# A gate projection by seven block products in two more token groups, with q of the last two batches weighted on ScalarE

One core of a Trainium2 chip. The metric is the device time of one execution in microseconds (us), median of several; smaller is better.

## The reference

Linear attention with a cosine weighting, then a SwiGLU block, all of it in one kernel:

```python
# q, k, v: (8 batches, 8 heads, 576 tokens, 64)
def phi(x, c, s):                       # c, s: cos and sin of pi/2 * position / 576
    r = np.maximum(x, 0.0)
    return np.concatenate([r * c, r * s], axis=-1)
kv  = einsum('bhsf,bhsd->bhfd', phi(k), v);  z = sum(phi(k), axis=2)
num = einsum('bhsf,bhfd->bhsd', phi(q), kv); den = phi(q) . z + 1e-6
x   = (num / den) -> (4608 tokens, 512)
g   = x @ w_gate                        # 512 x 1536
out = (silu(g) * (x @ w_val)) @ w_out   # 1536 x 512
```

## The kernel before

It works on nine groups of 512 tokens, 0 to 8. A group has a **gate stage** (gate and value projections, silu, product into `ht`; 12 slots, 0 to 11) and an **output stage** (4 slots, 12 to 15). The attention for coming groups is hung into these slots: `at(slot, function)` appends work, and every engine runs its instructions in the order in which the program emits them.

An ordinary gate stage has 12 blocks like this one, each with two of the eight PSUM banks (the buffers into which TensorE writes its sums, and which it can't use again until they have been read):

```python
def ffn_fc(tg, fc):
    # TensorE: 4 matmuls for the gate, 4 for the value, 512 tokens each
    # ScalarE: sg = silu(gate bank)
    # VectorE: ht[:, fc] = sg * value bank        (frees both banks)
```

Groups 7 and 8 (`GATE = (7, 8)`) make the gate by a scheme of seven products of half-size blocks instead of eight. The sums of blocks are made by VectorE, and intermediate results stay in PSUM:

```python
for u in range(3):                                     # [cut to the order of work]
    product(a, u, A11, B11, True)                      # TensorE
    nc.scalar.copy(out=b, in_=a)                       # ScalarE seeds bank b
    product(e, u, W3, X3, True);  nc.scalar.copy(out=m7, in_=e)
    V(...);  done()                                    # a value block; then the slot's work
    product(b, u, W2, X2, False)
    nc.vector.tensor_tensor(out=c, in0=m7, in1=b, op=ALU.add)      # must read b ...
    product(a, u, A12, B21, False);  silu(u, 1, 0, a)
    V(...);  done()
    product(b, u, W1, X1, False)                                   # ... before this writes b
    nc.vector.tensor_tensor(out=m7, in0=m7, in1=b, op=ALU.add)
    ...
    product(c, u, A22, X4, False); silu(u, 0, 0, c);  V(...);  done()
    mul(u, 0, 0); mul(u, 1, 0)                         # VectorE: silu times value
    product(b, u, W4, B22, False); silu(u, 1, 1, b)
    ...
```

A tile of 128 tokens of x (`a_tile2`) is 8 or 16 small matmuls and then three VectorE operations, `x_den`, `x_rec` and `x_mul` (the normalisation). The path of q of a batch b:

```python
def phi_q(b, g):                       # one of four head pairs
    o = raws[b, "q"][:, g]
    relu_op("act", o, o)                                          # ScalarE
    nc.vector.tensor_tensor(out=st[b, "q"][:, g], in0=o..., in1=tab, op=ALU.mult)   # weights
def qturn_dma(b, e):                   # transposes st[b, "q"] into phit[b], on SyncE's queue
    ...
def load_behind(b):
    nc.gpsimd.tensor_copy(out=hold2, in_=phit[b - 1][0:1, :, 0, 0, 0])  # waits for batch b-1's transposes
    load(b, "q")
    if b > 3:
        load_kv(b)
...
for b in range(2, B):
    s0 = SLOTS * (b - 1);  p0 = s0 - SLOTS         # SLOTS = 16: p0 is the start of group b - 2
    fs, tq = [p0 + 12, p0 + 12] + [p0 + 11 + i for i in range(2, 8)], (p0 + 15, p0 + 16)
    #        q: slots 12, 12, 13, 14; k and v: from slot 15 on; transposes of q: slots 15 and 16
    at(p0 + 3 if b < 5 else p0 + 1, lambda b=b: load_behind(b))
```

## Time and profile before

| | before |
|---|---|
| time, median (range) | 316.83 us (316.31 to 316.89) |
| TensorE busy | 98% of the span |
| VectorE, ScalarE busy | 73%, 46% |
| granted clock of TensorE | 0.998 |

In the rows of the windows further down, the columns are: start and end, length, busy time (and count) of PE (TensorE matmuls), PEld (weight loads), DVE (VectorE), ACT (ScalarE) and POOL (GpSimd), granted clock (1.00 is TensorE's full clock), DMA share, GB/s. In the order of time: start, length, engine, line, operation, count, and in brackets how long the engine had been idle and what ended that. In the lists of waits: what waited <- for what, us in total, how many times, the longest.

### The profile page before, as it was taken

The numbers are of one execution on the slowest core, as the hardware profiler recorded it, in microseconds if no ns is written. First come the engines' busy times: TensorE is split into PE (matmuls) and PEld (weight loads), VectorE is DVE, ScalarE is ACT, GpSimd is POOL, SyncE is SP. The second block draws the span as 40 slices with busy tenths as digits, with TensorE's granted clock in tenths as the row PEclk, the third lists the DMA queues.
The fourth block names the chain that finished last, engine by engine and source line by source line (L and its number), as shares of the span: only waits on it lengthen the run. The fifth ranks groups of instructions, "written<-read, shape, count | busy, mean of one in ns | idle before, by whom it ended". The sixth has DMA issues, their size and how long they took to land.

```text
span 314.5 us, 6775 instructions
## 1 busy us (share of the span) xinstructions
PE 307.5 (98%) x2696; PEld 189.7 (60%) x2696; DVE 228.2 (73%) x458; ACT 143.4 (46%) x264; POOL 36.0 (11%) x62
## 2 busy tenths in 40 slices
PE   8899999999999999999999999999999999999994
PEld 4597455455444585548654764577456866687673
DVE  7873777697678888587748786778779478946772
ACT  7554545763335346334543454335533345324530
POOL 7855102000200200030003000300000000000000
PEclk9999999999999999999999999999999999999999
DMA  7999999996897994989495979598951160014004
GB/s 268 217 198 197 206 205 138 226 133 99 143 208 114 150 145 110 148 119 196 100 153 75 200 144 154 73 192 135 164 86 35 40 145 17 20 38 98 0 2 133
DMA packets 74767, 41.07 MB, mean 131 GB/s; under 512 B 49904, under 2 KB 69872, under 8 KB 74736
## 3 DMA queue, kind: packets, MB, share of 16 engines
q1 hardware_dynamic: 51952, 22.55, 38.0%
q0 software_dynamic: 22192, 17.57, 37.2%
q10 hardware_dynamic: 592, 0.52, 0.5%
q8 instruction: 21, 0.34, 0.4%
q14 instruction: 10, 0.08, 0.1%
HBM read 37.75 MB, written 9.44 MB: 150 GB/s over the span
## 4 chain that ended last, share of the span: by engine, by line
PE 91%; DVE 5%; ACT 2%; issue 1%; ACTq 0%
PE banks L564 46%; PE banks L786 20%; PE banks L729 6%; PE banks L633 5%; PE banks L621 5%; PE banks L333 3%; PE banks L448 3%; DVE ht L638 1%; PE banks L494 1%; PE banks L430 1%; DVE v L287 1%; DVE sums L760 1%; DVE x L471 1%; PE banks L197 1%; PE banks L536 0%
## 5 line engine op out<-in xcount | busy, mean ns | idle before, releaser
L564 PE MATMUL banks<-xT,wg_sb 128*128 128x512 f16 (+2 forms) x368 | 86.6, 360 | 0.0
L564 PE MATMUL banks<-xT,wv_sb 128*128 128x512 f16 (+2 forms) x368 | 86.6, 360 | 0.0
L570 ACT ACTIVATE sg<-banks 128x512 bf16<-128x512 f32 (+2 forms) x92 | 51.5, 560 | 76.0 <-PE banks L564 74.0
L575 DVE TENSOR_TENSOR ht<-sg,banks 128x512 f16<-128x512 bf16 (+2 forms) x92 | 57.9, 637 | 29.7 <-PE banks L564 22.7
L564 PEld LDWEIGHTS <-wv_sb 128*128 128x128 f16 x368 | 35.5, 98 | 37.4
L564 PEld LDWEIGHTS <-wg_sb 128*128 128x128 f16 x368 | 33.9, 98 | 31.5 <-issue 0.2
L786 PEld LDWEIGHTS <-ht 128*128 128x128 f16 x336 | 32.5, 98 | 4.2
L786 PEld LDWEIGHTS <-sums 128*128 128x128 f16 x252 | 24.5, 98 | 4.2 <-issue 0.8
L633 PE MATMUL banks<-xT,wv_sb 128*128 128x512 f16 x96 | 24.3, 379 | 0.0
L283 DVE TENSOR_TENSOR r_q<-raw_q,tab 128x1152 bf16<-128x1152 bf16 x24 | 17.6, 754 | 7.4 <-ACT raw_q L266 7.1
L729 PE MATMUL banks<-wo_sb,ht 128*128 128x512 f16 x96 | 22.7, 379 | 0.0
L471 DVE TENSOR_TENSOR x<-banks,rec 128x512 f16<-128x512 f32 (+1 forms) x32 | 21.6, 674 | 1.3 <-PE banks L430 0.3
L786 PE MATMUL banks<-wo_sb,ht 128*128 128x256 f16 x168 | 20.6, 273 | 0.0
L287 DVE TENSOR_TENSOR v<-raw_v,tab 128x1152 bf16<-128x1152 bf16 x27 | 19.9, 751 | 0.5 <-ACT raw_v L849 0.5
L786 PE MATMUL banks<-wt_sb,sums 128*128 128x256 f16 x168 | 19.8, 273 | 0.1
L786 PE MATMUL banks<-wt_sb,ht 128*128 128x256 f16 x168 | 19.5, 273 | 0.0
L799 ACT ACTIVATE ob<-banks 128x512 f32<-128x512 f32 x14 | 8.4, 597 | 21.9 <-PE banks L786 21.9
L638 DVE TENSOR_TENSOR ht<-sg,banks 128x512 f16<-128x512 bf16 x24 | 15.5, 681 | 2.4 <-ACT sg L627 2.4
L266 ACT ACTIVATE raw_k<-raw_k 128x576 bf16<-128x576 bf16 (+1 forms) x25 | 17.1, 694 | 0.0
L998 POOL COPY hold<-phit 1x2 bf16<-1x2 bf16 x5 | 1.4, 287 | 129.3 <-DMA phit<-r_q 129.3
L760 DVE TENSOR_TENSOR sums<-ht 128x1024 f16<-128x1024 f16 (+1 forms) x28 | 15.5, 553 | 0.4
L266 ACT ACTIVATE raw_q<-raw_q 128x576 bf16<-128x576 bf16 x24 | 15.4, 675 | 0.0
(121 smaller groups left out, 334.6 us busy)
## 6 DMA issues: line engine op xcount, KB each, us to landing
out_dram<-ob SPq DMA_DIRECT2D x67, 128.0 KB, 2.5
raw_k<-in_k_dram POOLq DMA_DIRECT2D x7, 576.0 KB, 8.8
raw_q<-in_q_dram POOLq DMA_DIRECT2D x6, 576.0 KB, 6.0
raw_v<-in_v_dram POOLq DMA_DIRECT2D x6, 576.0 KB, 11.4
wo_sb<-in_moe_w_out_dram POOLq DMA_DIRECT2D x3, 512.0 KB, 12.8
wg_sb<-in_moe_w_gate_dram POOLq DMA_DIRECT2D x5, 256.0 KB, 9.4
wv_sb<-in_moe_w_val_dram POOLq DMA_DIRECT2D x5, 256.0 KB, 9.5
wo_sb<-in_v_dram SPq DMA_DIRECT2D x2, 576.0 KB, 4.0
```

The lines of the kernel that those rows point to most:

```text
L266: nc.scalar.activation(out=out, in_=in_, func=AF.Relu)
L283: nc.vector.tensor_tensor(out=st[b, "q"][:, g], in0=o.unsqueeze(2).to_broadcast([P, NC, 2, D]), in1=tab, op=ALU.mult)
L287: nc.vector.tensor_tensor(out=v2s[b == 1][:, g, :, :, 0:D], in0=(first if b == 0 and g == 0 else {"v": raw_of(b, "v")})["v"][:, g].unsquee ...
L471: nc.vector.tensor_tensor(out=st["x", t].rearrange("p (y e d) -> p e y d", e=2, d=D)[:, :, ys], in0=ps[:, :, 0:2 * J * D1].rearrange("p e ...
L564: nc.tensor.matmul(out=st["f", tg, fc, lo][i], lhsT=(wg_sb, wv_sb)[i][:, kc, fs], rhs=xT[tg][:, ts, kc], start=(kc == 0), stop=(kc == KC - 1))
L570: nc.scalar.activation(out=sg[:, 0:n], in_=st["f", tg, fc, lo][0], func=AF.Silu, scale=DOWN)
L575: nc.vector.tensor_tensor(out=ht[:, fc, r:r + n], in0=st.pop(("s", tg, fc, lo))[:, 0:n], in1=ps[1], op=ALU.mult)
L633: nc.tensor.matmul(out=val[u, i, w], lhsT=wv_sb[:, kc, fc * P:(fc + 1) * P], rhs=xT[tg][:, :, kc], start=(kc == 0), stop=(kc == KC - 1))
L638: nc.vector.tensor_tensor(out=ht[:, fc], in0=gates[u, w][:, i], in1=val.pop((u, i, w)), op=ALU.mult)
L729: nc.tensor.matmul(out=o_ps[t], lhsT=ht[:, fc, r:r + P], rhs=wo_sb[:, fc], start=(fc == 0), stop=(fc == FC - 1))
L760: nc.vector.tensor_tensor(out=o[:, lo:hi], in0=x[:, lo:hi], in1=y[:, lo:hi], op=op)
L786: nc.tensor.matmul(out=to[i][:, 0] if len(to) == 2 else to[0][:, i], lhsT=a[:, kc, i * P:(i + 1) * P], rhs=b[:, kc], start=first and kc == ...
```

## The change

Its intent: groups 5 and 6 use seven products too, which takes away an eighth of the gate's matmul work there. VectorE, which must do the extra additions, is relieved: q of batches 6 and 7 is weighted by ScalarE, by 18 relus a batch with a scale for each partition. The relus of k and the weighting of v of these batches move to the output stages, the copies of kv to ScalarE, one token sum to the output stage, and the tiles in front of seven-product groups to odd slots.

```diff
-    GATE = (7, 8)
+    PHI_ACT = 6
+    GATE = (5, 6, 7, 8)
...
+    def phi_q_part(b, c, w):
+        if (b, "q") not in st:
+            st[b, "q"] = rel.tile([P, G, NC, 2, D], BF16, name="r_q")
+        nc.scalar.activation(out=st[b, "q"][:, :, c, w], in_=raws[b, "q"][:, :, c], func=AF.Relu,
+                             scale=csk[:, c, w:w + 1])
...
-        for w, eng in enumerate((nc.scalar.copy, nc.vector.tensor_copy)):
+        for w, eng in enumerate((nc.scalar.copy, nc.scalar.copy if b - 1 in GATE else nc.vector.tensor_copy)):
...
-                token_sum(*((3, 0, 4) if u == 1 else (4, 0, 4)))
+            if u == 1:
+                token_sum(3, 0, 4)
...
-        token_sum(4, 4, 6)
+        token_sum(4, 0 if tg in GATE else 4, 6)
...
-        steps = [lambda b=b, g=g: phi_q(b, g) for g in range(G)]
+        steps = [lambda b=b, g=g: phi_q(b, g) for g in range(G)] if b < PHI_ACT else []
...
+            if b >= PHI_ACT:
+                for c in range(NC):
+                    at(p0 + 6 + c, lambda b=b, c=c: (phi_q_part(b, c, 0), phi_q_part(b, c, 1)))
+                fs = [p0 + 12, p0 + 12, p0 + 13, p0 + 15]
...
-            elif tg - 1 in GATE:
-                s = SLOTS * (tg - 1) + ((1, 2, 7, 9) if tg < 6 else (1, 2, 4, 7) if tg < 8 else (1, 2, 5, 6))[i]
+            elif tg in GATE:
+                s = SLOTS * (tg - 1) + ((1, 3, 7, 9) if tg < 6 else (1, 3, 5, 7))[i]
```

## The prediction

> **What bounds the kernel now.** I read the page first, then the chain that ended last, then the windows of each token group, then the order of time inside groups 4, 5 and 7.
>
> ```profile
> PE 307.5 (98%) x2696; PEld 189.7 (60%) x2696; DVE 228.2 (73%) x458; ACT 143.4 (46%) x264; POOL 36.0 (11%) x62
> PE 91%; DVE 5%; ACT 2%; issue 1%; ACTq 0%
> ```
>
> TensorE is busy for 98% of the span and holds 91% of the chain. The chain in order of time gives the group boundaries: group 4 runs from 152.70 us, 5 from 185.32, 6 from 217.83, 7 from 250.26, 8 from 281.13. The windows between them (length, then busy time of PE, PEld, DVE, ACT, POOL):
>
> ```profile
> 152.70:185.32 32.62, 32.59 (x294) 19.46 (x292) 24.14 (x46) 14.85 (x27) 2.40 (x4) 1.00 0.83 140
> 185.32:217.83 32.51, 32.48 (x285) 19.70 (x286) 24.74 (x47) 14.85 (x27) 2.91 (x4) 1.00 0.87 141
> 217.83:250.26 32.43, 32.43 (x295) 19.69 (x293) 23.13 (x45) 12.27 (x22) 0.00 (x0) 1.00 0.49 86
> 250.26:281.13 30.87, 30.37 (x251) 22.07 (x249) 22.95 (x45) 12.26 (x22) 0.00 (x0) 1.00 0.24 52
> ```
>
> Groups 4 to 6 are TensorE without a gap. Group 7, which already uses seven products, has 0.5 us of gaps, all of them waits for VectorE. So time comes only from matmul work taken away, as long as nobody makes TensorE wait. Who could? The change lets ScalarE read q earlier, so I looked at when q arrives (order of time, group 4, then group 5, then the q tile's landing times):
>
> ```profile
> 165.56 0.60 ACT L570 ACTIVATE sg<-banks 128x512 bf16<-128x512 f32 x1 [0.51 <-PE banks L564]
> 167.28 0.60 ACT L570 ACTIVATE sg<-banks 128x512 bf16<-128x512 f32 x1 [1.13 <-PE banks L564]
> ...
> 169.65 0.18 POOL L998 COPY hold<-phit 1x2 bf16<-1x2 bf16 x1 [31.01 <-DMA phit<-r_q]
> 170.10 0.74 POOL L131 DMA_DIRECT2D raw_q<-in_q_dram  x1 [0.28 <-PE banks L564]
> ...
> 179.11 1.25 ACT L266 ACTIVATE raw_q<-raw_q 128x576 bf16<-128x576 bf16 x2
> ```
> ```profile
> 201.50 0.73 POOL L998 COPY hold<-phit 1x2 bf16<-1x2 bf16 x1 [29.16 <-DMA phit<-r_q]
> 202.17 0.74 POOL L131 DMA_DIRECT2D raw_q<-in_q_dram  x1
> ```
> ```profile
> DMA to landing us min/median/max: 5.8/6.0/6.0
> ```
>
> The first line shown is the seventh silu of group 4 (slot 6). The load of batch 6's q goes out at 170.10, because the copy before it waits for the transposes of batch 5, and these stand in the queue behind the stores of group 3 (151.86 to 157.7). It lands at 170.10 + 6.0 = 176.1. Today ScalarE first touches it at 179.11 (slot 12): just in time. Batch 7's lands at 202.17 + 5.8 = 208.0, 22.7 us after group 5 began, and is first used at 211.62.
>
> **What the Trainium skill says.** "TensorE: Matmul & The Clock Gate", section "Architectural detail": the queues of ScalarE and VectorE are strict FIFO, so one instruction that waits for a DMA holds up all behind it. The trace agrees as far as it shows: in every group the order of time is the program's order. Same page, "What's actually happening": after about one idle window of 3.4 us TensorE's clock goes to half, and it takes a busy window to come back. In this trace the granted clock is 1.00 in every group, and 0.88 in the mean only in the last 4.5 us, when TensorE has nothing to do. No pause inside the run is long enough to test it. Same page, "Wait — 56ns, not 53.3ns?": N/2.4 GHz plus 2.5 ns for each matmul. The trace agrees: 48 matmuls of 512 columns took 10.36 us, 216 ns each, and 84 of 256 took 9.28 us, 110 ns each. "ScalarE: Activation LUTs", "What ACT_TABLE_LOAD costs": 186 ns + 0.833 ns per element, 93 ns more for a pointer scale, and 93 ns of overlap between neighbours. The 128x576 relu (675 ns; formula 666) agrees.
>
> **The change part by part.**
>
> Gate by seven products in groups 5 and 6. Out: 48 matmuls x 216 ns = 10.37 us. In: 84 x 108 ns = 9.07. TensorE saves 1.30 us a group, 2.6 in all. VectorE gains six adds of 0.69 and four token sums of 0.42 (5.8 us a group); ScalarE gains six copies of 0.58 (3.5). With 23 to 25 us and 12 to 15 us busy in 32.5, both can carry that by total. The two weight sums that stood in group 5 move earlier (0.95 us each, beside TensorE work).
>
> q of batches 6 and 7. Out: 4 relus x 0.675 = 2.7 us of ScalarE and 4 products x 0.754 = 3.0 of VectorE for each batch. In: 18 scaled relus of 256 elements at 186 + 93 + 213 = 492 ns, less 93 of overlap: 0.40 each, 7.2 us of ScalarE (estimates from the skill's formula). As an amount this is harmless. As a place it is not: the first pair stands at slot 6 of groups 4 and 5, the old ones stood at slot 12, and neither the load nor what it waits for is moved.
>
> Group 4, step by step. ScalarE finishes silu 6 at 166.2 and meets the first scaled relu, whose q lands at 176.1: 9.9 us blocked. TensorE goes on while it has banks: blocks 7, 8 and 9 (1.73 each, two banks each) and a tile (0.26, two banks) fill all eight at about 173.4. Silu 7 starts at 176.1 + 0.8 = 176.9, its product on VectorE ends at 178.2, and only then is there a bank: TensorE idle for about 5 us. VectorE then has eight operations in a row to go to the product of block 10 (products and token sums of 0.6, two tile normalisations of 1.06), which the output stage needs for its first matmuls: 178.2 + 5.7 = 183.9, against 175.8 now. **Loss 8.1 us.**
>
> Group 5, from its own start. q lands at +22.7 as before, since the whole chain of stores, transposes and load hangs on the end of group 4. Slot 6 comes after 14 product blocks (0.435), 7 value blocks (0.865), the key-value product (1.18) and three tiles (0.26): 14.1, with small waits 14.8. TensorE can do 2.0 us more (two product blocks, a value block, a tile) until +16.8 and then needs ScalarE's copy that seeds bank b. That comes after q and the first pair: 22.7 + 0.8 + 0.57 = 24.1. **Loss 7.3 us**; with the queue of relus behind it, 7.7; less the 1.3 saved, some 6.5 to 6.8 net.
>
> Cold clock. Both pauses are longer than one window, so I expect half speed for 3.4 to 6.8 us after each; where VectorE is the limit anyway this costs less. My estimate is 1 us in group 4 and 2 in group 5, from the page's window alone.
>
> Group 6 gains its 1.3 less about 0.3 of new waits: -1.0. Group 7: its tiles at slots 1 and 2 follow each other closely, and TensorE waits:
>
> ```profile
> 257.20 0.60 PE L621 MATMUL banks<-kvt,wgs_sb 128*128 128x256 f16 x4 [0.35 <-DVE x L471]
> 267.65 0.31 PEld L621 LDWEIGHTS <-wgs_sb 128*128 128x128 f16 x3 [0.36 <-issue]
> ```
>
> Its parts add up to 9.07 + 10.37 + 9.17 + 1.05 = 29.7 against 30.87 measured. Odd slots and one token sum (0.68) moved to the output stage should bring back half of it: -0.6. Group 8: 0. v in output stages: batch 6's v lands at 171.57 + 11.9 = 183.5; VectorE would meet it at about 181 if nothing else were late, but is 8 us late itself, so no wait is added.
>
> Sum: +8.1 + 6.7 + 3.0 - 1.0 - 0.6 = +16.2; I take two off for work that the queues let TensorE do after all: +14, that is **331 us**.
>
> **The rivals.** First, no block: if q came before slot 6, only the saving would be left, 316.83 - 2.6 - 0.6 + 0.5 = 314.1, within 2%. For it: the author tuned the slots, and ScalarE has half its time free. Against it: the landing of q follows from stores and transposes that the diff doesn't touch. Second, the block is there but mostly hidden: at the least, 9.9 less 5.4 of run-ahead in group 4 and 5.9 in group 5 stay, no cold clock, the savings in full: about 316.8 + 4.5 + 5.9 - 3.8 = 323.4. Third, VectorE becomes the bound of the gate stages: 12 products of 0.68, 6 adds of 0.69, 4 tiles of 1.06 and token sums of 3.3 make 19.9 us beside 20.5 to 21.7 of TensorE. It would eat the saving: 316 to 317. It is tight but under, and group 7 shows how small the waits are.
>
> **Range and chances.** 324 is the second rival with a little added, 338 the full sum with the cold clock at its longest in both groups. I give nine in ten to the block (slower by over 2% means above 323.2), one in eleven to the first or third rival, one in a hundred to over 2% faster: the whole matmul saving is under 1%.
>
> **What would show it.** In the profile of the changed kernel: ScalarE idle for some 10 us in group 4 and 8 in group 5 in front of the scaled relu, released by the q load; TensorE idle for 5 and 7 us there; granted clock under 1.00 in those slices; groups 4 and 5 near 41 to 43 and 39 to 41 us long, group 6 near 31.4, group 7 near 30.3. Wrong if the load of q is issued well before 165 us, or if ScalarE runs silus past the waiting relu; then the time is near 314.

## More of the kernel before

The weighted q (`r_q`) has one buffer, the raw q three.

## The result, and the profile after

The changed kernel took **337.35 us** (336.33 to 337.89, 4 runs) beside 316.82 us for the kernel before on the same chip: ratio 1.0648, 95% interval 1.062 to 1.0676. A ratio here is the mean time of one kernel's runs over that of the other's of the same rounds, so it is not quite the ratio of the medians.

First the page of the changed kernel, the lines that answer to those of the prediction, and the row of the clock in 40 slices:

```profile
PE 312.1 (93%) x2768; PEld 198.8 (59%) x2768; DVE 230.7 (69%) x462; ACT 159.9 (48%) x308; POOL 35.7 (11%) x62
PEclk9999999999999999999996999859999999999999
PE 72%; DVE 10%; DMA 9%; SPq 3%; ACT 3%; issue 2%; POOL 0%; DVEq 0%; POOLq 0%; ACTq 0%
```

TensorE's share of the chain has fallen from 91% to 72%. DMA and SyncE's queue hold 12% of it; before they did not appear. The granted clock has two dips. The windows of groups 4 to 7:

```profile
152.70:195.40 42.70, 35.77 (x295) 20.58 (x293) 24.97 (x48) 20.78 (x43) 2.40 (x4) 0.92 0.65 107
195.40:238.75 43.35, 35.22 (x323) 24.26 (x321) 26.32 (x49) 23.69 (x50) 2.41 (x4) 0.88 0.64 106
238.75:271.38 32.63, 32.17 (x330) 23.19 (x329) 23.46 (x45) 13.86 (x27) 0.00 (x0) 1.00 0.51 85
271.38:302.40 31.02, 29.83 (x245) 21.66 (x244) 22.79 (x44) 12.23 (x22) 0.00 (x0) 1.00 0.24 52
```

Groups 4 and 5 are 10 and 11 us longer than before. Group 6, which should have become shorter, is 0.2 us longer. (The last window ends 0.4 us before group 8 starts; group 7 takes 31.6 us.) The order of time in group 4:

```profile
170.18 0.17 POOL L1006 COPY hold<-phit 1x2 bf16<-1x2 bf16 x1 [31.51 <-DMA phit<-r_q]
170.63 0.75 POOL L132 DMA_DIRECT2D raw_q<-in_q_dram  x1 [0.28 <-PE banks L455]
...
176.26 0.91 ACT L290 ACTIVATE r_q<-raw_q,cs_all 128x256 bf16<-128x256 bf16 x2 [9.84 <-DMA raw_q<-in_q_dram]
177.07 0.57 ACT L577 ACTIVATE sg<-banks 128x512 bf16<-128x512 f32 x1
...
177.68 0.69 DVE L582 TENSOR_TENSOR ht<-sg,banks 128x512 f16<-128x512 bf16 x1 [10.29 <-ACT sg L577]
177.70 0.29 PE L455 MATMUL banks<-kv,phit 128*128 128x65 bf16 x4 [3.75 <-ACT sg L577]
...
180.06 1.86 PE L571 MATMUL banks<-xT,wg_sb 128*128 128x512 f16 x4 [1.28 <-DVE x L478]
```

The chain is to be read from the first line down. The q load leaves when it left before. ScalarE stands for 9.84 us in front of the first scaled relu (L290). The silu (L577) and VectorE's product (L582) stand behind it, and TensorE behind them for want of a bank. The last line has four 512-column matmuls in 1.86 us where four took 1.03 before. The clock in short windows tells why:

```profile
176.00:178.00 2.00, 0.29 (x4) 0.19 (x4) 0.32 (x1) 1.74 (x5) 0.00 (x0) 1.00 1.21 209
178.00:180.00 2.00, 0.37 (x4) 0.25 (x4) 1.93 (x6) 2.00 (x6) 0.00 (x0) 0.62 1.21 207
180.00:182.00 2.00, 1.94 (x5) 0.71 (x5) 2.00 (x5) 1.00 (x3) 0.00 (x0) 0.50 1.13 205
182.00:184.00 2.00, 2.00 (x6) 0.75 (x5) 1.63 (x5) 1.39 (x3) 0.00 (x0) 0.50 0.01 2
184.00:186.00 2.00, 2.00 (x8) 0.75 (x7) 1.36 (x3) 0.56 (x2) 0.00 (x0) 0.68 0.33 66
186.00:188.00 2.00, 2.00 (x20) 1.72 (x18) 1.53 (x3) 1.23 (x4) 0.00 (x0) 1.00 0.00 0
```

The column after POOL is the clock. It falls to a half at about 178.5, between the two short pieces of work in the pause, and is back at about 185.3, some 5 us after TensorE set to work again for good (180.06). In group 5 the same happens in the seven-product stage:

```profile
212.31 0.74 POOL L132 DMA_DIRECT2D raw_q<-in_q_dram  x1 [0.28 <-issue]
...
218.90 0.91 ACT L290 ACTIVATE r_q<-raw_q,cs_all 128x256 bf16<-128x256 bf16 x2 [7.45 <-DMA raw_q<-in_q_dram]
219.72 0.57 ACT L656 COPY banks<-banks 128x512 f32<-128x512 f32 x1
...
220.34 1.01 PE L628 MATMUL banks<-kvt,wgs_sb 128*128 128x256 f16 x4 [6.97 <-ACT banks L656]
```

Here it is the copy that seeds bank b (L656) for which TensorE waits 6.97 us.

### The profile page after: what moved, and what is told of

Its sections match the earlier page's. It is cut to its first block, busy times and chain, and to the rows that moved or that the text cites. A ratio compares the mean times of both kernels' runs of the same rounds, so it can differ in the third digit from the quotient of the medians.

```text
span 336.1 us, 6942 instructions
## 1 busy us (share of the span) xinstructions
PE 312.1 (93%) x2768; PEld 198.8 (59%) x2768; DVE 230.7 (69%) x462; ACT 159.9 (48%) x308; POOL 35.7 (11%) x62
## 4 chain that ended last, share of the span: by engine, by line
PE 72%; DVE 10%; DMA 9%; SPq 3%; ACT 3%; issue 2%; POOL 0%; DVEq 0%; POOLq 0%; ACTq 0%
PE banks L571 27%; PE banks L794 18%; PE banks L640 8%; PE banks L628 7%; PE banks L737 6%; DMA phit<-r_q 5%; DMA raw_q<-in_q_dram 4%; SPq L313 2%; DVE ht L645 2%; PE banks L340 2%; PE banks L455 2%; DVE v L294 1%; SPq L719 1%; DVE x L478 1%; PE banks L501 1%
## 5 line engine op out<-in xcount | busy, mean ns | idle before, releaser
L571 PE MATMUL banks<-xT,wg_sb 128*128 128x512 f16 (+2 forms) x272 | 63.8, 361 | 1.3 <-DVE x L478 1.3
L582 DVE TENSOR_TENSOR ht<-sg,banks 128x512 f16<-128x512 bf16 (+2 forms) x68 | 41.5, 620 | 32.2 <-PE banks L571 15.1
L571 PE MATMUL banks<-xT,wv_sb 128*128 128x512 f16 (+2 forms) x272 | 63.0, 358 | 0.0
L577 ACT ACTIVATE sg<-banks 128x512 bf16<-128x512 f32 (+2 forms) x68 | 37.1, 546 | 50.4 <-PE banks L571 47.2
L640 PE MATMUL banks<-xT,wv_sb 128*128 128x512 f16 x192 | 49.9, 387 | 0.3 <-DVE ht L645 0.3
L571 PEld LDWEIGHTS <-wg_sb 128*128 128x128 f16 x272 | 25.2, 99 | 23.8 <-issue 3.0
L645 DVE TENSOR_TENSOR ht<-sg,banks 128x512 f16<-128x512 bf16 x48 | 30.8, 680 | 6.0 <-ACT sg L634 6.0
L628 PE MATMUL banks<-kvt,wgs_sb 128*128 128x256 f16 x144 | 22.5, 280 | 8.0 <-ACT banks L656 7.0
L628 PEld LDWEIGHTS <-wgs_sb 128*128 128x128 f16 x192 | 18.2, 99 | 17.6 <-issue 11.0
L640 PEld LDWEIGHTS <-wv_sb 128*128 128x128 f16 x192 | 19.1, 100 | 14.8 <-issue 1.8
L634 ACT ACTIVATE sg<-banks 128x512 bf16<-128x512 f32 x36 | 20.4, 590 | 15.0 <-PE banks L628 14.9
L794 PEld LDWEIGHTS <-sums 128*128 128x128 f16 x252 | 24.6, 98 | 3.8 <-issue 1.0
L290 ACT ACTIVATE r_q<-raw_q,cs_all 128x256 bf16<-128x256 bf16 x36 | 16.1, 498 | 17.3 <-DMA raw_q<-in_q_dram 17.3
L737 PE MATMUL banks<-wo_sb,ht 128*128 128x512 f16 x96 | 22.7, 379 | 0.0
L794 PE MATMUL banks<-wo_sb,ht 128*128 128x256 f16 x168 | 20.6, 273 | 0.0
L294 DVE TENSOR_TENSOR v<-raw_v,tab 128x1152 bf16<-128x1152 bf16 x27 | 19.5, 750 | 0.5 <-ACT raw_v L857 0.5
L794 PE MATMUL banks<-wt_sb,sums 128*128 128x256 f16 x168 | 19.5, 273 | 0.0
L794 PE MATMUL banks<-wt_sb,ht 128*128 128x256 f16 x168 | 19.5, 273 | 0.0
```

The costliest lines, as they stand in the source:

```text
L294: nc.vector.tensor_tensor(out=v2s[b == 1][:, g, :, :, 0:D], in0=(first if b == 0 and g == 0 else {"v": raw_of(b, "v")})["v"][:, g].unsquee ...
L571: nc.tensor.matmul(out=st["f", tg, fc, lo][i], lhsT=(wg_sb, wv_sb)[i][:, kc, fs], rhs=xT[tg][:, ts, kc], start=(kc == 0), stop=(kc == KC - 1))
L577: nc.scalar.activation(out=sg[:, 0:n], in_=st["f", tg, fc, lo][0], func=AF.Silu, scale=DOWN)
L582: nc.vector.tensor_tensor(out=ht[:, fc, r:r + n], in0=st.pop(("s", tg, fc, lo))[:, 0:n], in1=ps[1], op=ALU.mult)
L628: nc.tensor.matmul(out=to[:, i], lhsT=a[:, c, 2 * u + i], rhs=x[:, :, c], start=first and i == 0 and c == 0, stop=c == KH - 1, skip_group_ ...
L634: nc.scalar.activation(out=gates[u, w][:, :, j * HT:(j + 1) * HT], in_=src, func=AF.Silu, scale=DOWN)
```

## The experiments

The lengths of the stages come from the order of time of TensorE (the first matmul of each stage), one profile each, in us. G is a gate stage, O the output stage before it:

| run | time, median | G4 | O5 | G5 | O6 | G6 | G7 |
|---|---|---|---|---|---|---|---|
| before | 316.6 to 316.8 | 23.3 | 9.5 | 23.0 | 9.4 | 23.2 | 21.5 |
| after | 337.35 | 33.5 | 9.2 | 33.6 | 9.7 | 23.5 | 22.4 |
| e1 q late | 325.60 | 24.3 | 10.2 | 26.9 | 9.9 | 26.2 | 22.4 |
| e2 gate only | 320.90 | 24.7 | 9.4 | 24.8 | 9.7 | 23.7 | 22.4 |
| e3 slots only | 316.60 | 23.3 | 9.4 | 23.0 | 9.4 | 23.3 | 21.7 |
| e4 q early | 319.79 | 24.6 | 9.2 | 23.8 | 9.7 | 23.8 | 22.4 |
| e5 q only | 334.89 | 31.9 | 9.2 | 31.8 | 9.2 | 23.2 | 21.4 |
| e6 zeros in the pause | 335.04 | 33.3 | 9.2 | 30.6 | 9.7 | 24.0 | 21.8 |
| e7 early, old slots | 320.58 | 24.3 | 9.2 | 24.5 | 10.1 | 24.1 | 21.7 |
| e8 early, even slots | 320.24 | 23.3 | 9.2 | 24.6 | 9.7 | 24.4 | 22.8 |
| e9 early, slot 7 | 318.35 | 23.3 | 9.7 | 23.8 | 10.1 | 24.1 | 21.7 |
| e10 no normalisation | 314.44 | 23.3 | 10.2 | 22.3 | 9.7 | 22.6 | 20.6 |

(O5 stands between G4 and G5.) G8, seven products with no attention work beside them, took 19.5 us in every one, which is the sum of its matmuls, 9.07 + 10.37.

### e5: the q part alone

```diff
 # the kernel before, with phi_q_part, without the old four steps of q, and
+            if b >= PHI_ACT:                       # PHI_ACT = 6
+                for c in range(NC):
+                    at(p0 + 6 + c, ... phi_q_part(b, c, 0), phi_q_part(b, c, 1))
+                fs = fs[4:]                        # k and v stay in their slots
```

> The kernel before with one part of the change: q of batches 6 and 7 by 18 scaled relus on ScalarE at slots 6 to 14; seven products in groups 7 and 8 only, tiles and v where they were. Theory (the relu that stands in front of a q not yet landed costs about 10 us in each of two groups, with or without the seven products): 333 to 338 us, groups 4 and 5 both near 42.5 us, granted clock near 0.92 in both. Rival (group 5 stalls in the changed kernel because its seven-product stage needs ScalarE's copies; with ordinary blocks the banks carry TensorE over it): 326 to 329 us, group 5 near 33 us.

Measured: 334.89 us (334.54 to 335.22), ratio 1.0576 (1.0561 to 1.0592). Groups 4 and 5 took 41.1 and 41.0 us, 8.3 and 8.6 more than before. Who waited for whom in groups 4 to 6, ScalarE (first line) and TensorE (the others):

```profile
ACT r_q L290 <- DMA raw_q<-in_q_dram: 18.3, 2, 9.2
...
PE banks L455 <- ACT sg L577: 10.0, 2, 5.1
PE banks L571 <- DVE x L478: 2.5, 2, 1.3
```

So the relus on ScalarE at these slots cost 18.3 us by themselves (16.9 of it in these two groups), without any new seven-product stage. The rival falls: ordinary blocks carry TensorE over only part of the wait, and it stood idle 5 us in each group. The clock was 0.92 in both, as expected. My figure of 42.5 us a group was 1.4 too high.

### e4: the cause taken away, the relus left in place

```diff
-        nc.gpsimd.tensor_copy(out=hold2, in_=phit[b - 1][0:1, :, 0, 0, 0])
-        load(b, "q")
+        if b >= PHI_ACT:                           # behind x of the group before, not behind q of the batch before
+            nc.gpsimd.tensor_copy(out=hold2, in_=xT[b - 2][0:1, 3, 0, 0:2])
+            load(b, "q")
+        nc.gpsimd.tensor_copy(out=hold2, in_=phit[b - 1][0:1, :, 0, 0, 0])
+        if b < PHI_ACT:
+            load(b, "q")
```

> The changed kernel, all in its place, but the q loads of batches 6 and 7 wait for the last turned tile of the group before instead of for the turned q of the batch before; k and v loads as they were. Theory (the lateness of the q load is the cause): q lands some 20 us earlier; what stays is that the single buffer of weighted q is read by the transposes until about 170 us in group 4 and 16 us into group 5, so ScalarE waits about 3.5 us in group 4 and 1 to 2 in group 5, TensorE nearly nothing; granted clock 1.00 throughout; 315.5 to 319 us. Rival (place or amount of the scaled relus is the cause): still above 325 us.

Measured: 319.79 us (319.59 to 322.05), ratio 1.0115 (1.0079 to 1.0151), granted clock 1.00 in the profiled run. The changed kernel lost 20.5 us against the kernel before; this one loses 3.2 against the kernel before of its own call, so 17.3 are back, with the same instructions in the same slots but for a one-row copy on GpSimd for each load. q now leaves at 150.71, and the second wait that had been hidden under the first is seen:

```profile
150.71 0.75 POOL L132 DMA_DIRECT2D raw_q<-in_q_dram  x1
...
169.82 0.31 PE L455 MATMUL banks<-kv,phit 128*64 128x65 bf16 x7 [1.09 <-DMA phit<-r_q]
...
169.93 0.91 ACT L290 ACTIVATE r_q<-raw_q,cs_all 128x256 bf16<-128x256 bf16 x2 [3.38 <-DMA phit<-r_q]
```

ScalarE waits 3.38 us for the transposes that still read the single weighted-q buffer (3.5 expected), and 0.29 us in group 5 (1 to 2 expected); the banks carry TensorE over that. TensorE's own 1.09 us, for a tile that needs the turned q, is another matter (e7). The time was 0.8 us above the range, so something besides the load keeps this kernel above the one before.

### e1: the relus after the landing

```diff
-                    at(p0 + 6 + c, lambda ...
+                    at(p0 + 12 + c // 3, lambda ...
```

> The changed kernel with the 18 scaled relus of batches 6 and 7 moved from slots 6 to 14 to slots 12 to 14 (three chunks of q a slot), all else as changed. Theory (ScalarE stands in line behind a q that has not landed): no wait of ScalarE for the q load over 1 us, granted clock 1.00 in every group, groups 4 and 5 back at about 32.6 and 31.5 to 32.5 us, time 314 to 318 us. Rival (the added 4.5 us of ScalarE work a batch, or the fuller gate stages, cost the time wherever they stand): still above 325 us.

Measured: 325.60 us (325.29 to 326.15), ratio 1.0279 (1.0262 to 1.0296). The theory's wait is gone: ScalarE waits nowhere for q in groups 4 to 6. But its time missed, and the measured one lies in the rival's range (above 325). One reason stands in the trace: 18 relus (7.5 us) now crowd into the output stage with four relus of k and the stage's own copies. TensorE's waits from group 4's output stage to group 6, then ScalarE's order of time where group 5 begins (187.2):

```profile
PE banks L628 <- ACT banks L656: 4.9, 2, 2.6
```
```profile
184.42 2.49 ACT L290 ACTIVATE r_q<-raw_q,cs_all 128x256 bf16<-128x256 bf16 x6
186.81 0.68 ACT L267 ACTIVATE raw_k<-raw_k 128x576 bf16<-128x576 bf16 x1
187.39 0.58 ACT L807 ACTIVATE ob<-banks 128x512 f32<-128x512 f32 x1
187.86 2.50 ACT L290 ACTIVATE r_q<-raw_q,cs_all 128x256 bf16<-128x256 bf16 x6
190.26 0.68 ACT L267 ACTIVATE raw_k<-raw_k 128x576 bf16<-128x576 bf16 x1
190.83 0.59 ACT L656 COPY banks<-banks 128x512 f32<-128x512 f32 x1
```

The seeding copy could start when the first product of the stage ends, at about 187.8; it comes at 190.83. The two waits of this kind make 4.9 of the 9.0 us lost. How much of the loss needs the relus at all is not separated here: e2, further down, loses 4.3 us without them. Group 5's 26.9 us also contain a clock dip that only the profiled run has (mean clock 0.992; the other three 0.999 to 1.000 and 0.5 to 0.8 us shorter): after a pause of 2.3 us the clock was at a half from about 192.8 to 196.2, while a pause of 2.6 us in group 6 brought none. So the relus have no room at slots 12 to 14 as they had none at slot 6: too early they stand before their data, late they are too many.

### e6: what the half clock costs

```diff
+            if tg == 5 and u == 2:
+                warm = take(1, fills=True)
+                for _ in range(28):
+                    nc.tensor.matmul(out=warm, lhsT=zeros, rhs=<zeros, 512 columns>, start=True, stop=True)
             product(b, u, W2, X2, False)
```

> The changed kernel with 28 matmuls of zeros (216 ns each, 6.0 us) put into TensorE's queue in group 5 at the point where it waits 7.0 us for ScalarE's copy; nothing else. Theory (the half clock after the pause costs 2 us and more by itself): the granted clock stays 1.00 in group 5 except for at most a us or two, the work from the copy to the output stage shrinks from 8.5 to 6 to 6.6 us, time 2.0 to 2.8 us under the changed kernel's 337.35: 334.5 to 335.4. Rival (after the pause ScalarE and VectorE set the pace, so the clock doesn't matter): 337 to 338.

Measured: 335.04 us (334.44 to 338.24), ratio 1.0602 (1.055 to 1.0653), 2.3 us under the changed kernel's median, though on another chip; the kernel before took 316.60 there and 316.82 here. One of the four executions took 338.24, and the intervals of the two ratios overlap, so it is the stage in the profile, and not the whole time, that shows the gain. The stretch from the copy to the output stage shrank from 8.5 us (220.34 to 228.86) to 5.6 (220.16 to 225.79). The same window of both, the changed kernel first:

```profile
220.00:226.00 6.00, 5.66 (x22) 3.19 (x22) 2.48 (x4) 3.41 (x8) 0.00 (x0) 0.50 0.99 166
```
```profile
220.00:226.00 6.00, 5.84 (x38) 3.71 (x38) 4.68 (x8) 5.50 (x13) 0.00 (x0) 1.00 0.85 141
```

22 matmuls at half clock, 38 at full. In group 5 the cold clock costs 2.9 us by itself. Group 4 could not be tested in this way, since all its banks are full in the pause.

### e3: the slots and the moved sum alone

```diff
-    PHI_ACT = 6
-    GATE = (5, 6, 7, 8)
+    PHI_ACT = 8                        # no q on ScalarE
+    GATE = (7, 8)
```

> The kernel before with only the odd tile slots and the moved token sum (seven products in groups 7 and 8 alone). My prediction gave this 0.6 us in group 7: 316.2 us. Theory after seeing the changed kernel (group 7 there took 31.0 us, not less than before): 316.5 to 317.2 us, no gain.

Measured: 316.60 us (316.33 to 316.76), ratio 0.9997 (0.9982 to 1.0012). No gain: the 0.6 us of the prediction are not there.

### e2: the seven products alone

```diff
-    PHI_ACT = 6
+    PHI_ACT = 8                        # q as before; GATE = (5, 6, 7, 8) stays
```

> The changed kernel with q of batches 6 and 7 weighted as before (relu on ScalarE, product on VectorE at slots 12 to 14, v one slot later as before); the seven products in groups 5 and 6, the tile slots, the moved token sum and the kv copies stay. Theory: the gate part alone is worth little, since groups 6 and 7 of the changed kernel gained nothing (32.63 and 31.0 us against 32.43 and 30.87): 315.5 to 317.5 us. Rival (a saving of 1.3 us in each of groups 5 and 6 arrives in full once nobody blocks): 314.0 to 314.5 us.

Measured: 320.90 us (320.77 to 321.05), ratio 1.0134 (1.0119 to 1.0149). Worse than either expected: not only does the saving fail to come, 4.3 us are lost. G4 lost 1.5 (24.72 against 23.26; the tile at slot 7 waiting 1.2 us for the turned q), G5 1.8, G6 0.5, G7 0.9. VectorE is busy in group 5's gate stage for 21.35 of its 24.8 us. One place, in order of time:

```profile
188.85 0.88 DVE L612 TENSOR_TENSOR kvt<-xT,kvt 128x512 f16<-128x512 f16 x2
...
189.33 0.61 PE L628 MATMUL banks<-kvt,wgs_sb 128*128 128x256 f16 x4 [0.62 <-DVE kvt L612]
```

TensorE waits for a sum of x blocks that came late in VectorE's queue, behind the last sum of gate weights (0.95 us) and an output copy (0.68).

### e7, e8 and e9: is a better arrangement near?

All three start from e4. e7 puts the tiles that are made in group 4's gate stage back to their old slots; e8 has in addition even slots in the later groups and the relus one slot later; e9 is e8 with the odd slots again.

```diff
 # e7
-((1, 3, 7, 9) if tg < 6 else (1, 3, 5, 7))[i]
+((5, 7, 9, 11) if tg < 6 else (1, 3, 5, 7))[i]
 # e8: in addition
-                    at(p0 + 6 + c, ...
+                    at(p0 + 7 + c, ...
-                                                           else (1, 3, 5, 7))[i]
+                                                           else (2, 4, 6, 8))[i]
 # e9: e8 with (1, 3, 5, 7)
```

> The run with the early q load (319.79 us) with the tiles of the first seven-product group back at slots 5, 7, 9, 11 of group 4; later groups keep odd slots. Theory: the tile at slot 7 of group 4 needs the turned q of batch 5, which lands about 170, and TensorE stood 1.1 to 1.2 us in front of it: gate stage of group 4 back from 24.5 to about 23.3 us, time 318.4 to 318.9. Rival (the wait is made up elsewhere): 319.5 to 320.

> As the run before it in this list, and the tiles of groups 6 to 8 at slots 2, 4, 6, 8 of the seven-product stages instead of 1, 3, 5, 7, and the scaled relus one slot later (7 to 15). Theory (the seven-product stages lose their saving because a tile at slots 3 and 7 puts its normalisation, 1.06 us of VectorE, in front of the add that frees bank b, and TensorE's next product into b waits): gate stages of groups 5, 6, 7 shrink by 0.5 to 1.0 us each from 23.8, 23.8, 22.4; time 315.5 to 317.5. Rival (VectorE's total or the banks set the pace, not the place of the tiles): no change, 318 to 319.

> The early q load, the first seven-product group's tiles at slots 5, 7, 9, 11 of group 4, the scaled relus one slot later (7 to 15), odd slots kept in the later groups. All waits for a transfer are out of it then. Theory (what is left over the kernel before is the seven-product stages of groups 5 and 6, which take 23.5 to 24 us where ordinary ones took 23.0 to 23.2): gate stage of group 4 at 23.3, time 318.0 to 319.3 us, so still not under the kernel before. Rival (the rest was the transfers after all): 314.5 to 316.

Measured: e7 320.58 us (320.23 to 321.55, ratio 1.0129), e8 320.24 (320.11 to 321.28, ratio 1.0123), e9 318.35 (318.26 to 319.20, ratio 1.0055, interval 1.0038 to 1.0072). In e7 the wait for the turned q is gone from TensorE, but others took its place: 0.9 us for a bank that VectorE held, while ScalarE still stood 3.1 us behind the transposes, and in the profiled run, the slowest of the four, 1.5 us for x. The expectation missed: the time lies above even the rival's 319.5 to 320. With the relus one slot later (e8, e9) G4 is back at 23.3. The even slots were a wrong idea: the three seven-product stages became 0.3 to 1.1 us longer than with odd ones, not shorter; in e8 TensorE's tiles waited 2.4 us in four places for banks that ScalarE had not read. e9 is the best correct form of the change, and it is 0.55% slower than the kernel before. (Not all waits for a transfer are out of it, as its expectation had it: ScalarE still stands 2.3 us behind the transposes once. TensorE waits for none.) No version of the change that beats the kernel before was found.

### e10: does VectorE keep the saving from coming?

Wrong on purpose (the output is far off: relative error 0.78). It is e9, but from tile 24 on the tile matmuls are made and not normalised:

```diff
     def x_of(t, ps):
+        if t >= 24:
+            st["x", t] = st["x", 23]
+            return
```

> Wrong on purpose: the run before it in this list, but the tiles of groups 6 to 8 (from tile 24 on) keep their matmuls and lose VectorE's three operations (1.06 us a tile); all of them send on the one x tile of number 23. Theory (VectorE, in order, carries tile normalisations, silu products and the adds between the products, and TensorE waits for the adds): with 4.2 us less of VectorE in a stage the saving appears: gate stages of groups 5, 6, 7 near their sum of parts, 21.7 to 22.2, 21.7 to 22.2 and 20.5 to 20.9 us; time 314 to 315.5 us. Rival (banks or ScalarE's copies set the pace): stages stay within 0.5 us of the run before it.

Measured: 314.44 us (313.86 to 315.07), ratio 0.9933 (0.9915 to 0.995). The gate stages of groups 5, 6 and 7, e9 first, then e10:

```profile
186.04:209.80 23.76, 22.97 (x238) 14.89 (x236) 18.88 (x37) 14.88 (x32) 1.66 (x3) 1.00 1.00 167
219.88:244.01 24.13, 23.01 (x247) 14.90 (x244) 18.19 (x36) 12.08 (x24) 0.00 (x0) 1.00 0.67 114
253.18:274.90 21.72, 21.33 (x166) 13.99 (x164) 17.34 (x35) 9.87 (x18) 0.00 (x0) 1.00 0.34 73
```
```profile
186.40:208.66 22.26, 22.01 (x238) 14.86 (x236) 15.19 (x25) 14.35 (x31) 1.66 (x3) 1.00 1.01 174
218.39:240.99 22.60, 22.23 (x247) 14.93 (x244) 14.41 (x24) 12.32 (x25) 0.00 (x0) 1.00 0.76 123
250.16:270.72 20.56, 20.56 (x167) 13.93 (x164) 13.65 (x23) 9.88 (x18) 0.00 (x0) 1.00 0.35 77
```

The matmul counts agree to one; 3.7 to 3.8 us of VectorE are gone from each stage (DVE is the figure after PEld's), and the stages are 1.5, 1.5 and 1.2 us shorter, though VectorE was busy for only 75 to 80% of them in e9. So VectorE's work is what eats most of the saving, here the normalisations, by their place in VectorE's queue or by the banks that they hold until they are done; the run takes both away together and does not part them. Whether other VectorE work of the same length would give as much back was not tried. Single waits don't tell it: those that the trace of e9 lists for TensorE inside the three stages add up to 1.7 us, while the stages are 5.8 us above the sums of their parts; the rest is time that the profile does not list as a wait. G7 is as the sum of its parts foretold (20.5). G5 and G6 stay 0.6 and 0.9 above theirs (21.7), 0.1 and 0.4 outside what I expected, so a smaller part of the waits is something else.

## Why the prediction was right

The mechanism was right and the time was within the range, near its upper end: 337.35 against 331 (324 to 338). That it is still inside owes something to luck: the top of the range was reasoned from the clock at its longest, and the saving that turned into a loss, the term that was wrong, was not in it. Step by step:

- **The block on ScalarE.** Foretold 9.9 us in group 4 and 7.9 in group 5 (q at +22.7, slot 6 at +14.8); measured 9.84 and 7.45 (in group 5 both came later: the relu started at +23.6, and ScalarE had stood since +16.2). A pair of scaled relus took 0.91 us (estimate 0.8), and the silu behind the first pair started at 177.07, though TensorE had filled its bank by about 167.5 (and that of the next silu by 171.4). That it is the cause was shown from two sides: the relus alone bring 18.3 us (e5), and the load alone, taken forward, gives 17.3 of 20.5 us back (e4).
- **TensorE's pauses.** Foretold about 5 and 7.3 us; measured 3.75 + 0.43 + 1.28 in group 4, after 1.5 for the turned q at slot 7, which was not foreseen, and 6.97 in group 5.
- **The half clock.** Foretold, but too small: 1 and 2 us. Its length was foretold rightly (3.4 to 6.8 us; measured 5.2 and 5.9 after the work had set in again). In group 5 it was 2.9 (e6). In group 4 it is not separated by an experiment: the output stage began at 186.1 where I had 183.9 without the clock, so 2.2 us for the clock and whatever else was off.
- **The saving of the seven products.** This term was wrong in sign. I had -1.3 inside group 5, -1.0 in group 6 and -0.6 in group 7. In the changed kernel, groups 6 and 7 became 0.2 and 0.7 us longer, and with the block gone (e9) G5 and G6 are 0.7 and 0.9 us longer than the ordinary ones. The third rival had the reason, and I put it aside because VectorE's total stayed under TensorE's time ("tight but under"). That compares totals, but TensorE waits for single additions and for banks, each behind whatever stands in VectorE's queue; e10 shows what that is worth. Nor did the odd slots help group 7 (e3). The reading behind that term was loose: of the 0.5 us of gaps in the old group 7, the trace puts only 0.35 us down to VectorE; the second line shown is a weight load that waited for nothing that the profile shows.
- **"Two off for work that the queues let TensorE do after all".** There was no such work. The sum as worked out was 333. It has a slip of 0.3: 7.7 less 1.3 is 6.4, not 6.7. By groups, the profiled run stands above the sum by 0.9 us in group 4, 2.2 in group 5, 1.2 in group 6 and 1.3 in group 7 (5.6 us, of which the profiled run's own excess over the median is 0.5). In groups 6 and 7 that is the saving that did not come; in group 5, 0.9 is the clock and the rest is not taken apart.
- **v in output stages.** I foretold no wait for the transfer, and none is in the changed kernel. There is a small wait of another kind: 0.39 us of TensorE in group 5's output stage for an output sum behind v's products.

The first rival (no block) and the second (mostly hidden, 323.4) fall by the trace itself. Losses do not add up: q alone costs 18.3 us and the seven products alone 4.3, both together 20.5, as one would expect where a wait lies inside a longer one; no run takes that apart.

## What to carry to other kernels

Before you move work on an in-order engine to an earlier slot, look up when its input lands and what releases that transfer; it costs what all behind it lose. Here a pair of relus of 0.9 us, six slots forward, cost about 8.5 us a group where the relus were tried alone. Spare time on an engine, as a share, does not tell whether an addition in the path of the bound engine comes in time: count what stands before it in the queue, and which buffers that work holds. And a pause of TensorE can be dearer than its length: the one of 7 us cost 2.9 us more at half clock.

## What the Trainium skill lacked or had wrong

- "TensorE: Matmul & The Clock Gate" ("What's actually happening") has the clock back after at least one busy window of about 3.4 us, and budgets one. Here half clock lasted about 5.2 us after work had resumed in group 4 (180.06 to about 185.3) and about 5.9 us in group 5 (220.34 to about 226.2). Both are more than one window and less than two. That fits the page's remark that the window runs freely; a budget of one was too small in both pauses.
- No page says whether products of zeros hold that clock. In the one place tried, they did: 28 of them kept it at 1.00 through the pause and after it (e6), where it had been 0.50 in the changed kernel.
